# Identity products in TensorE's waits, later places for weight conversions, and two swaps at a handover

## The chip, the cores and the metric

One core of one Trainium2 chip runs the whole kernel in a single launch. The time is device microseconds of that core, as a median of runs. A core has five engines that run side by side, each through its own instructions in order: TensorE (PE, with its weight loads as PEld), VectorE (DVE), ScalarE (ACT), GpSimd (POOL) and SyncE (SP), which here issues most of the transfers. The transfers themselves run on 16 DMA engines.

## The reference

Three layers in sequence, on 4 batches of 448 tokens, 12 heads of 64:

```python
scores = q @ k.T / sqrt(64)                       # per batch and head
scores = einsum('bhij,hg->bgij', scores, w_pre)   # mix the heads
attn = softmax(scores - scores.max(-1))           # over j
attn = einsum('bhij,hg->bgij', attn, w_post)      # mix the heads again
x = (attn @ v), heads side by side                # 1792 x 768

h = x @ w_in                                      # 768 x 2048
x = (h - tanh(h)) @ w_out                         # 2048 x 768

logits = x @ phi                                  # 8 experts x 4 slots = 32
d = softmax(logits, over tokens); slot_input = d.T @ x
slot_out[e] = relu(slot_input[e] @ w1[e]) @ w2[e] # 768 x 1024 x 768, e < 8
out = softmax(logits, over slots) @ slot_out
```

All arrays are float32 on the chip, but for `w_in` and `w_out`, which come as float64 and are converted by the kernel on its own engines, as pairs of 32-bit words.

## The kernel before, in words

**Stage 1, attention** (`talking_heads`). Queries are cut into chunks of 120 (four a batch, the last of 88), and each chunk into slots of 10 queries with all 12 heads: 180 slots, 45 a batch. The main loop takes one step per slot. In step s it regroups the scores of slot s + 4 by a DMA from `S` to `D`, mixes the heads of slot s (`premix`, L317), normalizes slot s - 1, and mixes slot s - 3 again (`postmix`, L353). Everything else is planned into steps ahead of the loop, in the table `at`: scores of the next chunk ("head"), turns of k and q, products with v (`values`, L371), and transfers ("load"). The turns of the next batch's k (`k_pair`) lie in a stretch of 11 steps ahead of the batch: from `start[m - 1] - D_AHEAD` on, steps 20 to 30, 65 to 75 and 110 to 120. Their loads are up to six steps earlier.

Into the same steps go the 64 conversions of `w_in` and `w_out`, in pieces of 128 x 384. A conversion is a load by SyncE (L84 or L90), an absolute value on ScalarE (`absolute`, L46), four VectorE instructions (`exponent`, `head`, `tail`), an addition on GpSimd (L67) and a store by SyncE (L116). The planner walks through the pieces and chooses for each the step of the absolute value (a), of the exponent (x), the head (h) and the tail (e): a is the one of the steps t0 and t0 + 1 with the least planned load on ScalarE, where t0 is the later of `due` and of the head step of the piece before. The load is planned at the later of a - 4 and two steps after the tail of the piece three before, as there are three buffers.

**Handover.** The second function, `moe_and_slots`, is a generator: stage 1 calls `next` on it at the end of each of its last steps. There it loads and splits (`split_w`, `split_x`) the first weights and x into a rounded part and a rest, runs the first two products (`product`, L707), and begins their gates (`gate_act` on ScalarE, `gate_first` and `gate_last` on VectorE).

**Stage 2.** 64 steps, 16 blocks of hidden columns f for each of 4 batches: product of step t, gate of t - 1, turn of t - 2 (`turn_g`). In the first batch each step also loads and splits a block of `w_in`, saves it (`save_w`) for the other batches, and turns pieces of `w_out` (`turn_w`, two for each f, in all 32). The dictionary `pieces` says how many in which step; in steps 5, 9, 13 and 16 four turned blocks are folded with `phi` (`fold_first`, `fold_last`). The turns use the two banks r0 and r1 in alternation.

**Between stage 2 and the experts** (lines 1020 to 1076): the gate of the last step, its turn, the last logits (`logits`, L805), their mix (`mix_t`, L816), the exponentials (`slot_exp`), their turn (`slot_turn`, L872), the sums over tokens into slots (`slot_sum`, L881), `dt` (L1050), and the slots' inputs `si` (L1061) through `w_out`. **The experts** follow, with 32 weight loads of 1536 KB each (L647). Each load waits in a queue for a free "home" in SBUF: `give` adds one, `take` returns one after its use, and both call `load_expert`, which issues the next load. PSUM has eight banks; `h0`, `h1`, `h2` hold the products of three steps in turn.

Of the kernel before, what the change touches and what calls it, by code (L numbers as in the profile page):

```python
# [16 lines left out]
NB, NH, SEQ, HD = 4, 12, 448, 64  # L17
# [4 lines left out]
CHUNK = 120  # L22
# [96 lines left out]
def attention_chunks():  # L119
    out = []  # L120
    for b in range(NB):
        for i0 in range(0, SEQ, CHUNK):
            n = min(CHUNK, SEQ - i0)
            w = -(-n // IB)
            out.append((b, i0, n, [(o, len(range(o, n, w))) for o in range(w)]))
    return out
# [20 lines left out]
def talking_heads(tc, ident, q, k, v, w_pre, w_post, xd, box, follow):  # L147
    nc = tc.nc
    R = IB * NH
    chunks = attention_chunks()  # L150
    NC = len(chunks)
    slots = [(n, kk) for n in range(NC) for kk in range(len(chunks[n][3]))]
    NS = len(slots)
    D_AHEAD = 4
# [228 lines left out]
    start = [sum(len(c[3]) for c in chunks[:n]) for n in range(NC + 1)]  # L383
    at = {}

    def plan(kind, s, *a):
        at.setdefault((kind, s), []).append(a)
# [3 lines left out]
    def calm(kind, lo, hi):  # L391
        return min(range(lo, hi + 1), key=lambda s: (load[kind][s], s))
# [41 lines left out]
    pieces = box["early"]  # L434
    done = [0, 0, 0]
    t = 2
    for i, j in enumerate(pieces):
        due = 3 + i * (NS - D_AHEAD - 14) // len(pieces)
        t0 = max(t, due)
        a = calm("act", t0, t0 + 1)  # L440
        x = calm("dve", a + 1, a + 1 + (a <= due))
        load["dve"][x] += 0.54
        h = calm("dve", x, x + 1)
        load["dve"][h] += 0.47
        e = calm("dve", h, h + 1)
        load["dve"][e] += 0.74
        load["act"][a] += 0.41
        t = h
        done.append(e)
        plan("load", max(a - 4, done[i] + 2), cv.load, j)  # L450
        plan("act", a, cv.absolute, j)
        plan("dve", x, cv.exponent, j)
        plan("dve", h, cv.head, j)
        plan("dve", e, cv.tail, j)
        plan("load", e + 2, cv.store, j)
# [11 lines left out]
    warm = ps.tile([128, 128], FP32, tag="t", name="warm", bufs=2)  # L467
# [85 lines left out]
def moe_and_slots(tc, ident, xd, wi, wo, wo4, wis, consts, w1, w2, out, box):  # L553
    nc = tc.nc
# [3 lines left out]
    NE, _, F1 = w1.shape  # L558
# [27 lines left out]
    def bank(tag, shape, name):  # L586
        return bank_pool[tag].tile(shape, FP32, tag=tag, name=name)

    def r32(ap):
        return ap.bitcast(F32R)  # L590
# [14 lines left out]
    def unit(t):  # L605
        return ring[t % 3 if t < LAST else t % 2]
# [10 lines left out]
    def give(x, last=False):  # L617
        free.append((x, last))
        load_expert()
# [4 lines left out]
    def load_expert():  # L624
        if not queue or not free:
            return
        key = queue.pop(0)
        home = free.pop(0)
        x = home[0]
        kind, t = key  # L630
        if kind == "o":
            nc.sync.dma_start(out=x, in_=wo4[t])
        else:
            e, part = divmod(t, 4)
            i = part % 2
            if part < 2:
                n = KD // 2
                src = w1[e].rearrange("(p a) f -> p a f", p=128)[:, i * n:(i + 1) * n, :]
            else:
                src = w2[e].rearrange("(p a) f -> p a f", p=128)  # L640
                if by_column(e):
                    n = KF1
                    src = src[:, :, i * HALF:(i + 1) * HALF]
                else:
                    n = KF1 // 2
                    src = src[:, i * n:(i + 1) * n, :]
            nc.sync.dma_start(out=x.rearrange("p (a f) -> p a f", a=n), in_=src)  # L647
        ex_tiles[key] = home
# [22 lines left out]
    def split_w(t, eng):  # L671
        if t < NF:
            w = unit(t)
            nc.scalar.activation(out=r32(w[:, :, 0]), in_=w[:, :, 1], func=ACTF.Copy)
            eng.tensor_tensor(out=r32(w[:, :, 1]), in0=w[:, :, 1], in1=w[:, :, 0], op=ALU.subtract)  # L675
# [44 lines left out]
    def gate_act(t, beside=None):  # L720
        hp = hps[t]
        if t > 1:
            mem["sq"] = {t: bank(f"q{t % 2}", [128, SEQ], "sq")}
        sq, qd, mk, g = temps_of(t)
        nc.scalar.activation(out=sq, in_=hp, func=ACTF.Square)  # L725
        nc.scalar.activation(out=qd, in_=sq, func=ACTF.Square, bias=tshift)
        if beside:
            beside()
        nc.scalar.activation(out=g, in_=hp, func=ACTF.Tanh)
        nc.scalar.activation(out=mk, in_=sq, func=ACTF.Relu, bias=tlimit, scale=-1.0)  # L730
# [8 lines left out]
    def gate_last(t):  # L739
        hp = hps.pop(t)  # L740
        sq, qd, mk, g = temps_of(t)
        nc.vector.scalar_tensor_tensor(out=hp, in0=qd, scalar=TG_C, in1=hp, op0=ALU.mult, op1=ALU.mult)
        nc.vector.copy_predicated(out=g, mask=mk.bitcast(I32), data=hp)
# [10 lines left out]
    def turn_g(t):  # L754
        b, f = divmod(t, NF)
        if f % NG == 0:
            tok[b, f // NG] = quads.pop(0)
        g = g_of(t)
        x = turn_bank([JP, NR, 128], "gt")
        for r in range(NR):  # L760
            nc.tensor.transpose(out=x[:, r, :], in_=g[:, r * JP:(r + 1) * JP], identity=ident)  # L761
        i = f % NG
        dst = tok[b, f // NG][:JP].rearrange("p (r f) -> p r f", r=NR)[:, :, i * 128:(i + 1) * 128]
        nc.scalar.activation(out=dst, in_=x, func=ACTF.Copy)
# [44 lines left out]
    def logits_out(b):  # L809
        s = keep.tile([128, SEQ], FP32, tag="lp", name="lp")  # L810
        nc.scalar.activation(out=s, in_=lg.pop(b), func=ACTF.Copy)
        lp[b] = s

    def mix_t(b):
        xt = bank("lg", [128, SEQ], "lT")
        nc.tensor.matmul(xt, lhsT=sel.rearrange("p g s -> p (g s)"), rhs=lp[b], start=True, stop=True)  # L816
        lg[b] = xt
# [7 lines left out]
    def slot_exp(b):  # L825
        xt = lg.pop(b)
        nm = keep.tile([128, 1], FP32, tag="nm", name="nm")
        ng = keep.tile([128, 1], FP32, tag="ng", name="ng")
        et = keep.tile([128, SEQ], FP32, tag="et", name="et")
        sb = keep.tile([128, 1], FP32, tag="sb", name="sb")  # L830
        a = None
        nc.vector.tensor_reduce(out=nm, in_=xt, op=ALU.max, axis=AX.X)
        if b:
            nc.vector.tensor_tensor(out=nm, in0=nm, in1=run_m, op=ALU.max)
        nc.vector.tensor_scalar(out=ng, in0=nm, scalar1=-1.0, scalar2=None, op0=ALU.mult)
        nc.scalar.activation(out=et, in_=xt, func=ACTF.Exp, bias=ng, accum_out=sb)
        if b:
            a = keep.tile([128, 1], FP32, tag="al", name="al")
            nc.scalar.activation(out=a, in_=run_m, func=ACTF.Exp, bias=ng)
        es_in[b] = (a, et)  # L840
        runs[b] = (nm, sb)

    def slot_run(b):
        nm, sb = runs.pop(b)
        if b:
            nc.vector.tensor_scalar(
                out=run_s, in0=run_s, scalar1=es_in[b][0], scalar2=sb, op0=ALU.mult, op1=ALU.add)
        else:
            nc.vector.tensor_copy(out=run_s, in_=sb)
        nc.vector.tensor_copy(out=run_m, in_=nm)  # L850
# [17 lines left out]
    def slot_turn(b):  # L868
        a, et = es_in[b]
        xe = turn_bank([JP, NR, NSL], "etp")  # L870
        for r in range(NR):
            nc.tensor.transpose(out=xe[:, r, :], in_=et[:NSL, r * JP:(r + 1) * JP], identity=ident[:NSL, :NSL])  # L872
        es = keep.tile([JP, NR, NSL], FP32, tag="es", name="es")
        nc.scalar.activation(out=es, in_=xe, func=ACTF.Copy)
        es_in[b] = (a, es)
# [14 lines left out]
    pieces, folds = {}, {5: 0, 9: 1, 13: 2, 16: 3}  # L890
    todo = [(f, hf) for f in range(NF) for hf in range(2)]
    for n in range(3, NF + 1):
        m = 3 if n in (3, 4, 14, 15) else 2
        pieces[n], todo = todo[:m], todo[m:]

    def step(t):
# [89 lines left out]
    save_w(1)  # L986
    load_w(4)
    yield
    gate_act(1)
    yield  # L990
    split_w(2, nc.vector)
    while not box.get("go"):
        yield
    gate_first(1)
# [28 lines left out]
    xz = thp.tile([128, 2 * EXB], FP32, tag="xb", name="ex")  # L1023
    for i in range(2):
        give(xz[:, i * EXB:(i + 1) * EXB])
    gate_act(t - 1)
    gate_first(t - 1)
    turn_g(t - 2)
    gate_last(t - 1)
    turn_g(t - 1)  # L1030
    logits(b, NQ - 1)
    logits_out(b)
    temps.close()
    tmp = whole.enter_context(tc.tile_pool(name="m_tz", bufs=1, side="right", reuse_waits="tile"))
    give(tmp.tile([128, EXB], FP32, tag="tz", name="ex"))
    mix_t(b)
    slot_exp(b)
    slot_turn(b)
    slot_run(b)
    dgs = [bank(n, [128, FB], "sp") for n in ("h0", "h1", "q0", "q1")]  # L1040
    sr = keep.tile([128, NSL], FP32, tag="sr", name="sr")
# [15 lines left out]
    for k in range(NQ):  # L1057
        w = take(("o", k), NG)
        for hf in range(2):
            for g in range(NG):  # L1060
                nc.tensor.matmul(  # L1061
                    si[hf][NSL * g:NSL * g + NSL, :], lhsT=dgT[:, k * NG + g, :],
                    rhs=w[:, g, hf * HALF:(hf + 1) * HALF], start=(k == 0), stop=(k == NQ - 1))
# [245 lines left out]
```

## Time and profile before

| what | before |
|---|---|
| median of 3 runs | 962.18 us (961.09 to 964.81) |
| the profiled execution's own time | 964.55 us |
| its span, first to last instruction | 962.8 us |
| TensorE busy | 916.1 us, 95% |
| VectorE, ScalarE, GpSimd busy | 566.3, 571.1, 265.8 us |
| mean granted clock of TensorE | 0.973 |
| transfers | 230.22 MB, mean 239 GB/s |

The shares are over the whole span, and stages differ: about 490 us of attention, 340 us of stage 2, then 130 us of slots and experts. Matmuls are pipelined, so a busy TensorE is not one at its peak. The granted clock is a share of 2.4 GHz; 0.50 is 1.2 GHz.

### The profile page before, as it was taken

The numbers are of one execution on the slowest core, as the hardware profiler recorded it, in microseconds if no ns is written. First come the engines' busy times: TensorE is split into PE (matmuls) and PEld (weight loads), VectorE is DVE, ScalarE is ACT, GpSimd is POOL, SyncE is SP. The second block draws the span as 40 slices with busy tenths as digits, with TensorE's granted clock in tenths as the row PEclk, the third lists the DMA queues.
The fourth block names the chain that finished last, engine by engine and source line by source line (L and its number), as shares of the span: only waits on it lengthen the run. The fifth ranks groups of instructions, "written<-read, shape, count | busy, mean of one in ns | idle before, by whom it ended". The sixth has DMA issues, their size and how long they took to land.

```text
span 962.8 us, 19390 instructions
## 1 busy us (share of the span) xinstructions
PE 916.1 (95%) x6952; PEld 678.8 (71%) x6952; DVE 566.3 (59%) x1251; ACT 571.1 (59%) x1291; POOL 265.8 (28%) x467
## 2 busy tenths in 40 slices
PE   8899999989999999999989999999999999799985
PEld 6677777767777777777777777778778867444532
DVE  4576667766677766676455665667767666520103
ACT  4787777767776777776565675556556645401113
POOL 1464455544455545555422330000000000000000
PEclk9999999999999999999999999999999999868988
DMA  5897667977578876775548976796465448779997
GB/s 139 232 257 208 189 204 223 229 208 209 186 227 232 214 219 203 219 227 163 182 164 289 319 262 229 281 380 242 157 217 169 144 138 308 284 306 417 423 392 275
DMA packets 139634, 230.22 MB, mean 239 GB/s; under 512 B 58324, under 2 KB 118804, under 8 KB 134932
## 3 DMA queue, kind: packets, MB, share of 16 engines
q1 hardware_dynamic: 136976, 216.40, 69.5%
q10 hardware_dynamic: 2564, 12.60, 3.3%
q8 instruction: 56, 0.92, 0.4%
q14 instruction: 38, 0.31, 0.1%
HBM read 154.25 MB, written 36.18 MB: 198 GB/s over the span
## 4 chain that ended last, share of the span: by engine, by line
PE 81%; DMA 9%; ACT 4%; DVE 3%; issue 2%; POOL 0%; SPq 0%; ACTq 0%; POOLq 0%; DVEq 0%
PE hp L707 21%; PE pm L317 14%; PE tm L353 13%; PE vx L371 7%; PE sc L286 6%; PE gt L761 3%; PE h L1092 2%; PE sp L881 2%; PE so L1131 2%; DMA ex<-in_moe_w_dram 2%; DMA f<-in_moe_w_in_dram 2%; DMA rg<-wi 2%; DMA rg<-wis 2%; PE lgp L805 1%; PE tz L1110 1%
## 5 line engine op out<-in xcount | busy, mean ns | idle before, releaser
L353 PEld LDWEIGHTS tm<-wk,e 120*112 120x112 f32 (+1 forms) x1440 | 174.9, 178 | 70.8 <-issue 56.5
L319 DVE TENSOR_REDUCE mx<-pm 120x1 f32<-120x448 f32 x180 | 112.0, 622 | 124.5 <-PE pm L317 123.2
L317 PE MATMUL pm<-D,wpre 120*120 120x448 f32 x360 | 175.1, 569 | 6.8 <-ACT e L326 4.1
L353 PE MATMUL tm<-wk,e 120*112 120x120 f32 (+1 forms) x1440 | 177.5, 267 | 0.9 <-POOL wk L343 0.9
L356 ACT ACTIVATE aT<-tm 112x480 f32<-112x480 f32 x180 | 105.1, 584 | 111.3 <-PE tm L353 111.2
L343 POOL TENSOR_SCALAR wk<-wpost,rv 120x120 f32<-120x120 f32 x180 | 127.7, 709 | 136.1 <-PE tm L353 110.5
L707 PE MATMUL hp<-xa,rg 128*128 128x448 f32 x576 | 138.5, 380 | 0.6 <-POOL rg L675 0.6
L707 PE MATMUL hp<-xb,rg 128*128 128x448 f32 x576 | 133.5, 377 | 1.7 <-DMA rg<-wis 1.7
L707 PEld LDWEIGHTS hp<-xb,rg 128*128 128x128 f32 x576 | 103.9, 188 | 23.8 <-issue 14.1
L326 ACT ACTIVATE e<-pm,mx 120x448 f32<-120x448 f32 x180 | 113.4, 630 | 6.0 <-DVE rv L338 3.6
L707 PEld LDWEIGHTS hp<-xa,rg 128*128 128x128 f32 x576 | 102.3, 189 | 19.5 <-issue 11.5
L1103 POOL MEMSET tq<- 128x256 f32 x8 | 2.4, 311 | 339.0 <-PE sp L881 267.9
L294 ACT ACTIVATE S<-sc 120x448 f32<-120x448 f32 (+1 forms) x186 | 90.5, 543 | 3.1 <-PE sc L286 3.0
L371 PE MATMUL vx<-aT,vn 112*64 112x120 f32 (+1 forms) x1536 | 85.3, 265 | 1.8 <-DVE xs L376 1.8
L725 ACT ACTIVATE sq<-hp 128x448 f32<-128x448 f32 x62 | 32.8, 529 | 90.0 <-PE hp L707 89.7
L735 DVE SCALAR_TENSOR_TENSOR qd<-qd,sq 128x448 f32<-128x448 f32 x62 | 38.5, 621 | 79.3 <-ACT mk L730 79.0
L371 PEld LDWEIGHTS vx<-aT,vn 112*64 112x64 f32 x1536 | 75.0, 138 | 7.9 <-DVE xs L376 1.9
L317 PEld LDWEIGHTS pm<-D,wpre 120*120 120x120 f32 x360 | 51.6, 183 | 29.9 <-ACT e L326 15.9
L286 PE MATMUL sc<-khi,qT 64*120 64x448 f32 (+1 forms) x384 | 69.1, 388 | 0.8 <-DVE qT L269 0.8
L332 POOL TENSOR_SCALAR rv<-ss 120x1 f32<-120x1 f32 x180 | 41.2, 229 | 103.6 <-ACT e L326 92.3
L67 POOL TENSOR_TENSOR fa<-fa,f 128x384 f32<-128x384 f32 x64 | 65.9, 1030 | 5.3 <-DVE rv L338 0.2
L46 ACT ACTIVATE fa<-f 128x384 f32<-128x384 f32 x64 | 35.8, 559 | 18.8 <-DMA f<-in_moe_w_in_dram 15.3
(166 smaller groups left out, 1256.1 us busy)
## 6 DMA issues: line engine op xcount, KB each, us to landing
ex<-in_moe_w_dram SPq DMA_DIRECT2D x28, 1536.0 KB
D<-S SPq DMA_DIRECT2D x172, 210.0 KB
rg<-wis SPq DMA_DIRECT2D x34, 768.0 KB
f<-in_moe_w_in_dram SPq DMA_DIRECT2D x32, 384.0 KB
f<-in_moe_w_out_dram SPq DMA_DIRECT2D x32, 384.0 KB
wis<-rg ACTq DMA_DIRECT2D x16, 768.0 KB
rg<-wis SPq DMA_DIRECT2D x28, 384.0 KB
wi<-fa SPq DMA_DIRECT2D x32, 192.0 KB
```

The lines of the kernel that those rows point to most:

```text
L67: eng.tensor_tensor(out=out, in0=bits(a), in1=bits(p), op=ALU.add)
L286: nc.tensor.matmul(xs[e][0][:ni], lhsT=qT[n][s, l, p, :ni], rhs=kt[s], start=(i == 0), stop=(i == 2))
L294: nc.scalar.activation(out=dst, in_=xs[e][0][:ni], func=ACTF.Copy)
L317: nc.tensor.matmul(x[:r], lhsT=wpre[:r, :m, :], rhs=D_t.pop(s)[:r], start=True, stop=True)
L319: nc.vector.tensor_reduce(out=mx[:r], in_=x[:r], op=ALU.max, axis=AX.X, negate=True)
L326: nc.scalar.activation(out=e[:r], in_=pp_t.pop(s)[:r], func=ACTF.Exp, bias=mx_t.pop(s)[:r], accum_out=ss[:r])
L332: nc.gpsimd.tensor_scalar(out=rv[:r], in0=ss_t.pop(s)[:r], scalar1=EPS, scalar2=None, op0=ALU.add)
L343: nc.gpsimd.tensor_scalar(out=wk[:r], in0=wpost[:r], scalar1=ss_t.pop(s)[:r], scalar2=None, op0=ALU.mult)
L353: nc.tensor.matmul(x[:, c, :, :m], lhsT=e[:r, c * JP:(c + 1) * JP], rhs=wk[:r, :, :m], start=True, stop=True)
L356: nc.scalar.activation(out=attn_t[n][:, :, :, c0:c0 + m], in_=x[:, :, :, :m], func=ACTF.Copy)
L371: nc.tensor.matmul(x[64 * e:64 * e + 64, i, :ni], lhsT=nat_v[b, h // NP][:, h % NP, c, :], rhs=a[:, c, h, :ni], start=(c == 0), stop=(c == ...
L707: nc.tensor.matmul(hp, lhsT=r32(w[:, m, hl, cs]), rhs=r32(x_of(b, c, l)), start=(c == 0 and i == 0), stop=(c == KD - 1 and i == 2))
```

## The change

Four edits. The conversions of stage 1 get their due steps from a list of "quiet" steps, which leaves out the 11 steps in which the next batch's k is turned; the due steps inside that list are spread evenly, every second step. One turned piece of `w_out` moves from step 3 to step 5 of stage 2. In the generator, `split_w(2)` and `gate_act(1)` change places: the split is made one step of stage 1 earlier, the gate one later. And between stage 2 and the experts, TensorE multiplies the identity by itself 30 times, in five groups, into bank `h1`; the results are not read.

```diff
@@ talking_heads
     t = 2
+    busy = set()
+    for m in range(1, NC - 1):
+        if chunks[m][1] + CHUNK >= SEQ:
+            busy |= set(range(start[m - 1] - D_AHEAD, start[m - 1] - D_AHEAD + 11))
+    quiet = [x for x in range(4, NS - D_AHEAD - 11) if x not in busy]
     for i, j in enumerate(pieces):
-        due = 3 + i * (NS - D_AHEAD - 14) // len(pieces)
+        due = quiet[i * len(quiet) // len(pieces)]
         t0 = max(t, due)
@@ moe_and_slots
     for n in range(3, NF + 1):
-        m = 3 if n in (3, 4, 14, 15) else 2
+        m = 3 if n in (4, 5, 14, 15) else 2
         pieces[n], todo = todo[:m], todo[m:]
@@
     load_w(4)
     yield
+    split_w(2, nc.vector)
+    yield
     gate_act(1)
-    yield
-    split_w(2, nc.vector)
     while not box.get("go"):
         yield
@@
         give(xz[:, i * EXB:(i + 1) * EXB])
+    idle = bank("h1", [128, 128], "warm")
+
+    def warm(n):
+        for _ in range(n):
+            nc.tensor.matmul(idle, lhsT=ident, rhs=ident, start=True, stop=True)
+
+    warm(5)
     gate_act(t - 1)
     gate_first(t - 1)
     turn_g(t - 2)
+    warm(15)
     gate_last(t - 1)
     turn_g(t - 1)
     logits(b, NQ - 1)
     logits_out(b)
+    warm(2)
     temps.close()
     tmp = whole.enter_context(tc.tile_pool(name="m_tz", bufs=1, side="right", reuse_waits="tile"))
     give(tmp.tile([128, EXB], FP32, tag="tz", name="ex"))
     mix_t(b)
+    warm(7)
     slot_exp(b)
     slot_turn(b)
+    warm(1)
     slot_run(b)
```

## Rows read from the trace of the kernel before

**Rows 1.** The page: the chain that ended last, by engine.
```profile
PE 81%; DMA 9%; ACT 4%; DVE 3%; issue 2%; POOL 0%; SPq 0%; ACTq 0%; POOLq 0%; DVEq 0%
```

**Rows 2.** Windows: length, busy time (instructions) of each engine; clock, DMA share, GB/s.
```profile
core 0: us, PE busy (x) PEld busy (x) DVE busy (x) ACT busy (x) POOL busy (x), PEclk, DMA share, GB/s
...
140.00:160.00 20.00, 18.94 (x167) 14.21 (x163) 13.05 (x35) 14.22 (x36) 10.04 (x18) 1.00 0.74 211
...
180.00:200.00 20.00, 17.57 (x150) 13.63 (x148) 13.65 (x34) 13.87 (x35) 9.32 (x17) 0.96 0.95 239
200.00:220.00 20.00, 20.00 (x158) 14.88 (x155) 13.09 (x34) 13.35 (x34) 8.37 (x16) 0.96 0.72 196
...
300.00:320.00 20.00, 19.46 (x174) 15.07 (x175) 14.81 (x35) 15.05 (x39) 11.81 (x20) 1.00 0.94 237
...
880.00:900.00 20.00, 20.00 (x248) 10.38 (x242) 0.57 (x3) 1.19 (x2) 0.93 (x3) 1.00 1.00 419
```

**Rows 3.** Timeline of ScalarE: start, length, what, [idle before, its end].
```profile
162.80 0.56 ACT L46 ACTIVATE fa<-f 128x384 f32<-128x384 f32 x1
...
188.85 0.55 ACT L46 ACTIVATE fa<-f 128x384 f32<-128x384 f32 x1 [2.88 <-DMA f<-in_moe_w_in_dram]
...
195.24 0.54 ACT L46 ACTIVATE fa<-f 128x384 f32<-128x384 f32 x1 [2.71 <-DMA f<-in_moe_w_out_dram]
...
312.36 0.55 ACT L46 ACTIVATE fa<-f 128x384 f32<-128x384 f32 x1 [3.76 <-DMA f<-in_moe_w_in_dram]
```

**Rows 4.** Timeline of SyncE, the issuing of transfers in stage 1.
```profile
158.32 0.45 SPq L90 DMA_DIRECT2D f<-in_moe_w_in_dram  x1
...
183.17 0.62 SPq L116 DMA_DIRECT2D wo<-fa  x1
183.89 0.39 SPq L90 DMA_DIRECT2D f<-in_moe_w_in_dram  x1
...
188.85 0.37 SPq L84 DMA_DIRECT2D f<-in_moe_w_out_dram  x1
```

**Rows 5.** Timelines of VectorE and TensorE at the handover.
```profile
502.03 0.96 DVE L675 TENSOR_TENSOR rg<-rg 128x768 fp32r<-128x768 f32 x1 [1.84 <-ACT rg L674]
...
503.30 1.44 PE L371 MATMUL vx<-aT,vn 112*64 112x88 f32 x32 [1.77 <-DVE xs L376]
...
518.97 0.55 PE L774 MATMUL wt<-ident,ex 128*128 128x128 f32 x3 [0.92 <-ACT ex L778]
```

**Rows 6.** The chain in order of time, at the start and behind the handover.
```profile
1.43 4.64 PE warm L472 x20
...
508.90 7.81 DMA rg<-wi
```

**Rows 7.** Timeline of TensorE, an earlier slot sum and the stretch after stage 2.
```profile
616.52 1.07 PE L881 MATMUL sp<-tq,es 112*32 112x512 f32 x8
...
831.85 0.62 PE L761 MATMUL gt<-ident,g 128*112 128x128 f32 x4 [1.29 <-DVE g L743]
...
835.96 1.07 PE L761 MATMUL gt<-ident,g 128*112 128x128 f32 x4 [3.48 <-DVE g L743]
...
839.35 1.86 PE L816 MATMUL lT<-lp,sel 128*128 128x448 f32 x2 [0.66 <-ACT lp L811]
843.06 0.58 PE L872 MATMUL etp<-ident,et 32*112 32x32 f32 x4 [1.86 <-ACT et L836]
844.00 6.67 PE L881 MATMUL sp<-tq,es 112*32 112x512 f32 x32 [0.37 <-ACT es L874]
```

**Rows 8.** Windows between stage 2 and the experts.
```profile
836.00:844.00 8.00, 5.12 (x18) 1.76 (x18) 1.64 (x8) 2.32 (x6) 0.00 (x0) 0.50 1.01 432
844.00:850.00 6.00, 6.00 (x31) 1.36 (x32) 2.22 (x4) 0.00 (x0) 0.50 (x2) 0.50 0.47 199
847.00:851.00 4.00, 4.00 (x24) 0.98 (x16) 1.75 (x3) 0.00 (x0) 0.56 (x2) 0.61 0.01 3
851.00:855.00 4.00, 3.97 (x31) 3.83 (x30) 0.50 (x1) 0.00 (x0) 0.00 (x0) 0.82 0.81 261
```

**Rows 9.** Timeline of SyncE: the loads into the homes that the slot sums free.
```profile
850.79 0.81 SPq L647 DMA_DIRECT2D tq<-in_moe_w_dram  x2
```

## The prediction

> **What bounds the kernel now.** I read the chain of the whole run first: four fifths of it is TensorE and a tenth waiting for transfers, so a change counts where TensorE stands still or where a transfer ends last [rows 1]. Then the windows of 20 us. In stage 1 (to about 490 us) TensorE has no idle time in most of them; the exceptions are few: 1.06 us in 140 to 160, 2.43 us in 180 to 200, 0.54 us in 300 to 320. The granted clock of 0.96 in the two windows of 180 to 220 is 0.8 us less time at full speed in each, 1.6 us together. In 880 to 900 the DMA engines are at 1.00 of their time: the experts' weights set the pace there, not TensorE [rows 2].
>
> The waits of stage 1 come from one instruction. ScalarE takes the absolute value of a converted block (L46) in order, and stands until the block's load has landed: 2.88 and 2.71 us at the 25th and 26th conversion, 3.76 us at the 43rd, nothing at the 21st [rows 3]. SyncE issued those loads as late as 188.85 for a use at 195.24, 6.4 us; the quiet one was issued at 158.32 and used without a wait at 162.80, 4.5 us [rows 3, 4]. While the next batch's k is fetched, a load takes some 2 us longer.
>
> **Stage 1, the new places of the conversions.** The change keeps 64 conversions, their instructions and DMAs, and moves only their due steps. I worked through the loop of lines 437 to 455 with the costs written in it. Before, a due step comes every 2.5 steps; after, every second step outside three stretches (20 to 30, 65 to 75, 110 to 120). But `due` is only a lower bound: the start is at or after `max(t, due)`, and `t` is the head step of the conversion before, two or three steps after its start. At a due step in every two, the starts fall behind and can't catch up. So worked out, the starts around the second stretch are 60, 62, 64, 66, 69 (before: 60, 62, 64, 66, 69, 72, 74), around the third 105, 107, 109, 111, 114 (before: 105, 107, 109, 113, 115, 118). So the two that stalled, at 64 and 66, stay where they are, and the third stretch gets the same pair, 109 and 111, that it does not have now. The ones taken out (72, 74, 115, 118) are none of those that waited. Also, a load must wait for the buffer of the conversion three before, so at this pace its lead over its use shrinks to one step for 37 conversions (12 before).
>
> The prices. Second stretch: one more store and load stand ahead of the load for step 66 on SyncE's queue; such a pair is 183.17 to 184.28, 1.1 us [rows 4]. With the gap behind it I add 1.2 us to the stall, as if SyncE never stood idle there. The regroup transfers behind it on that queue are late by as much. Bounds: nothing is added and the stall goes, -2.43 and -1.6 for the clock, or +3 (two more pairs and their transfers). Third stretch: like the second now, 2.43 + 1.2 - 0.54 = 3.1 us, and half of the clock's 1.6 (whether the clock falls depends on how long TensorE stands), +3.9; bounds -0.5 and +5.5. First stretch (starts at 13, 15, 17, 19, then none to 32): +0.5, bounds 0 and +2.4. The other close starts: the wait in 140 to 160 is what such a series costs where it begins, 1.06 us [rows 2]; later ones in a series waited for nothing at the 21st conversion, so +0.4, bounds 0 and +2. VectorE, GpSimd and ScalarE have the same work, some 27% closer in the quiet steps; they are busy 13 to 15, 8 to 12 and 13 to 15 of 20 us [rows 2], which hides it. Sum of stage 1: 1.2 + 3.9 + 0.5 + 0.4 = **+6.0 us**.
>
> The Trainium skill ("DMA: Bandwidth & Descriptors", sections Bandwidth and Latency) gives a fixed cost of about 2 us and 341 GB/s at 1 MB; an estimate from it for 384 KB is 3.2 us, and by it a lead of one step would do and this term would be 0. The trace does not agree where k is fetched: 6.4 us stand from issue to use there [rows 3, 4].
>
> **The handover to stage 2.** The split of w 2 now goes ahead of gate 1 on ScalarE. Before, its VectorE half starts at 502.03, since its copy stood behind gate 1; the copies of the last values stand behind it and TensorE waits 1.77 us for them [rows 5]. After, the copy fits ahead of gate 1, whose input is not ready earlier anyway, so I take the 1.77 off. Moving the turn of one piece from step 3 to step 5 removes a wait of 0.92 us in step 4 [rows 5]. What is late next: the load of the next w, 7.81 us long, on which ScalarE stands ahead of the copies that free the turns' banks [rows 6]. It lands when the queue of weight loads and saves before it has drained, and these don't shrink; ScalarE stands until then whether TensorE came 1.8 us earlier or not. In step 5 the fold now comes right behind the third turned piece and may wait for its copy. So most is given back: **-0.4 us**, bounds -2.7 (all kept) and +0.5 (nothing kept, and a wait before the fold).
>
> **The identity products.** Between the last product and the experts TensorE waits 1.29, 3.48, 0.66, 1.86 and 0.37 us [rows 7], and behind the second works at half clock: 5.12 us busy in 836 to 844, 6.00 in 844 to 850, clock 0.50 in both [rows 8]. The 5, 15, 2, 7 and 1 products go into just these waits, into a bank that nothing else uses until `dgs`. Ten of them took 4.64 us at the start of the kernel, 0.46 each [rows 6]. That is a price at the lower level: at 0.50 the mix of 448 columns takes 1.86 us [rows 7, 8], or 0.53 for 128. At the upper level it is 0.23, and the five groups take 1.16, 3.48, 0.46, 1.62 and 0.23 us: all fit, the second one just. Bounds 0.23 and 0.46. At the first wait the clock is still full (four transposes take 0.62 us behind it and 1.07 behind the second [rows 7]), and TensorE would be busy through all five, as in 880 to 900, where the clock is 1.00 [rows 2], so I take 0.23.
>
> Then the work in 836 to 844 halves, up to -2.5, and so do the slot sums: 32 instructions in 6.67 us at half clock, 8 of an earlier batch in 1.07 at full, ends included [rows 7], so some 3.4, -3.3. About -5.6 us at the slot sums' end. That alone is not the gain, since the end is set by weights. But the slot sums release two homes, and their loads are issued at 850.79 [rows 9], while the DMA engines have stood empty since 847: share 0.01 in 847 to 851, 0.81 in 851 to 855 [rows 8], 3.96 + 0.76 = 4.7 us lost. Issued at 845.2, they follow on the loads before without a gap; some 0.9 us are in hand. From there on the stream is full in the rows [rows 2], and what feeds it comes as much earlier. The term is **-4.7 us**; the rest of 5.6 is hidden by the stream. Bounds: -4.9 and 0 (if the clock falls all the same).
>
> **The sum.** -4.7 - 0.4 + 6.0 = +0.9 us on the profiled execution's 964.55 us (a span of 962.8 and 1.75 around it), which lies 2.4 above the median. Moved to the median of 962.18: **963 us**. What a measurement of this kernel can tell from no change is about 0.5%, 957.4 to 967.0.
>
> **The rivals.**
> - *The conversions cost nothing, or their stalls go* (chance 0.31). For it: the quiet load of 4.5 us was in time with a lead of one step [rows 3, 4], the DMA engines have more room without four conversions per stretch, and waits of up to 3.76 us on ScalarE cost TensorE only 0.54 [rows 2, 3]. Then -4.7 - 0.4 = 957; with the stall of 180 to 200 and its clock gone too, -4.1 more, 953. By the Trainium skill's figure above it is this case. Against it: the starts 64 and 66 do not move.
> - *Every stretch stalls as the second does now, and each close series costs its 1 us* (0.17; the one that ends slower). The place is L46 with a lead of one step during the fetch of k; it decides once loads there take 6.4 us or more. First +2.4, second +3, third +5.5, series +2: 12.9 - 5.1 = +7.8, 970 us. For it: the starts 109 and 111. Against it: the load of the 43rd, late by 3.76 us, took only 0.54 from TensorE [rows 2, 3].
> - *The change doesn't hold the clock or its products run at the lower level* (0.09). At 0.46 the second group takes 7 us in a wait of 3.48 and pushes the chain; the term of -4.7 goes to 0 or above: 968 us. Against it: the clock is full when the first group starts [rows 7].
>
> **How the numbers follow.** My case has 0.43, with its own range of 958 to 967. The range over the cases leaves out the rivals' ends: 953.5 to 970. Faster by over 0.5%: the first rival, 0.30. Slower: the second and part of the third and of mine, 0.27. Within: 0.43.
>
> **What would show it.** In the changed profile: conversions at the 23rd and 24th place with ScalarE idle 2 us or more before L46 (step 64 and 66), and a TensorE gap of over 2 us near 315 where there is 0.54 now; no such gaps would prove the first rival. The gap of 1.77 before the last values gone, the load of w landing near 516 still. Granted clock 1.00 from 831 to the slot sums' end, the two loads issued 13 to 14 us behind the transposes at the first wait (19 now), and the DMA engines never empty from there to the last weights. What would make it wrong above all: stage 1 of 4 us more or less.

## The result, and the profile after

| | median (lowest to highest) | runs |
|---|---|---|
| before | 961.63 us (957.89 to 964.81) | 6 |
| after | 967.49 us (965.85 to 970.64) | 6 |

The ratio is 1.0068, with a 95% interval of 1.0038 to 1.0097 (that of the two medians is 1.0061): the changed kernel is slower. The time lies in the forecast range, 4.5 us above the forecast itself; of the three directions it took the one that had been given 0.27. The profiled execution of the changed kernel has a span of 968.6 us, 5.8 more than before.

Where the span changed can be followed by three marks: the start of stage 2's product 0, its product 16 (the first that reads `xb`), and the end of its last product.

| profiled execution | product 0 starts | product 0 to 16 | product 16 to the last one's end | from there to the end |
|---|---|---|---|---|
| before | 490.60 | 99.95 | 240.00 | 132.27 |
| after | 498.80 | 103.78 | 239.87 | 126.14 |

So stage 1 is 8.2 us later, the handover loses 3.8 and the tail gains 6.1. Forecast were +6.0, -0.4 and -4.7. These are differences of two single executions; how far such marks vary stands in the table behind the experiments.

Stage 1. The waits of ScalarE ahead of L46, SyncE's issues that they hang on (L84 loads from `w_out`, L90 from `w_in`), and TensorE's gaps in the changed kernel, in timelines:
```profile
55.08 0.54 ACT L46 ACTIVATE fa<-f 128x384 f32<-128x384 f32 x1 [3.36 <-DMA f<-in_moe_w_in_dram]
...
186.72 0.55 ACT L46 ACTIVATE fa<-f 128x384 f32<-128x384 f32 x1 [4.00 <-DMA f<-in_moe_w_out_dram]
...
192.59 0.54 ACT L46 ACTIVATE fa<-f 128x384 f32<-128x384 f32 x1 [2.02 <-DMA f<-in_moe_w_in_dram]
...
311.93 0.55 ACT L46 ACTIVATE fa<-f 128x384 f32<-128x384 f32 x1 [5.29 <-DMA f<-in_moe_w_in_dram]
```
```profile
46.46 0.39 SPq L90 DMA_DIRECT2D f<-in_moe_w_in_dram  x1
...
181.65 0.42 SPq L84 DMA_DIRECT2D f<-in_moe_w_out_dram  x1
...
185.29 1.26 SPq L90 DMA_DIRECT2D f<-in_moe_w_in_dram  x1
```
```profile
56.75 1.35 PE L317 MATMUL pm<-D,wpre 120*120 120x448 f32 x2 [3.38 <-ACT e L326]
...
313.61 1.10 PE L317 MATMUL pm<-D,wpre 120*120 120x448 f32 x1 [2.65 <-ACT e L326]
```
A load issued at 181.65 lets ScalarE go on at 186.72, one issued at 185.29 at 192.59: 5.1 and 7.3 us, the second more than the 6.4 of [rows 3, 4]. The load of the 5th conversion, issued at 46.46, lets it go on at 55.08: 8.6 us, the longest of those that it stood for. The stall near 313 is there, as forecast, and one near 56 that I had put at half a microsecond. The signs named were waits at the 23rd and 24th conversion (starts 64 and 66); they are 2.02 and 1.58 us. The longest wait in both later stretches is one start earlier than I had worked out: 4.00 us at 186.72 (start 62) and 5.29 us at 311.93 (start 107). Windows of the changed kernel, same columns as [rows 2]:
```profile
180.00:200.00 20.00, 16.35 (x131) 12.04 (x130) 13.70 (x33) 12.12 (x32) 9.05 (x17) 1.00 0.96 250
300.00:320.00 20.00, 17.35 (x129) 12.98 (x128) 13.04 (x33) 11.52 (x30) 9.14 (x16) 0.91 0.83 225
320.00:340.00 20.00, 18.96 (x167) 14.60 (x168) 14.29 (x34) 13.65 (x35) 10.10 (x19) 1.00 0.59 168
510.00:520.00 10.00, 6.92 (x55) 6.07 (x52) 3.40 (x8) 4.29 (x7) 3.65 (x2) 0.90 0.93 278
520.00:530.00 10.00, 10.00 (x47) 8.86 (x47) 4.86 (x9) 4.81 (x9) 1.85 (x1) 0.75 0.68 232
836.00:844.00 8.00, 7.76 (x47) 6.91 (x47) 4.82 (x9) 4.20 (x8) 0.00 (x0) 1.00 0.12 28
844.00:850.00 6.00, 5.50 (x47) 4.24 (x45) 2.97 (x5) 2.27 (x5) 0.00 (x0) 1.00 0.96 401
850.00:870.00 20.00, 18.60 (x163) 11.72 (x162) 5.78 (x14) 2.06 (x6) 0.56 (x2) 0.99 0.97 390
```
In 180 to 200 TensorE is idle for 3.65 us in four gaps of at most 1.48 us (2.43 us in one gap before), and the clock stays at 1.00; in 300 to 320 for 2.65 in one gap (0.54 before), and there it falls.

The handover. The wait of 1.77 us of [rows 5] is gone. In its place TensorE stands 3.08 us for the output weights `wo`, which the chain of waits shows with a transfer of 6.82 us. Timeline of TensorE, then the chain in order of time:
```profile
519.01 0.87 PE L779 MATMUL wt<-ident,ex 128*128 128x128 f32 x3 [3.08 <-DMA ex<-wo]
```
```profile
512.05 6.82 DMA ex<-wo
```
In the kernel before, the same turns in the timeline of TensorE, and two windows:
```profile
510.76 0.52 PE L774 MATMUL wt<-ident,ex 128*128 128x128 f32 x3 [1.07 <-DMA ex<-wo]
```
```profile
510.00:520.00 10.00, 8.33 (x51) 7.33 (x52) 5.36 (x10) 6.91 (x13) 3.67 (x2) 1.00 0.83 289
520.00:530.00 10.00, 9.62 (x62) 6.93 (x64) 5.87 (x11) 6.23 (x12) 1.85 (x1) 1.00 0.82 271
```
SyncE began to issue the four loads of `wo` 13.25 us behind the start of product 0, and they were there at 20.2; before, it began at 15.2 behind it and they were there at 20.2 as well (TensorE waited 1.07 us for them at 510.76). So the earlier issue brought nothing. The DMA engines were busy 0.96 of the time meanwhile (512 to 519), which I take for the reason; no run tried it. Then the clock falls: 0.90 and 0.75 in the windows above, where before it was 1.00.

The tail, timeline of TensorE and the two loads of [rows 9]:
```profile
843.84 3.51 PE L1035 MATMUL warm<-ident 128*128 128x128 f32 x30
...
853.67 3.64 PE L886 MATMUL sp<-tq,es 112*32 112x512 f32 x32
```
```profile
857.42 0.80 SPq L652 DMA_DIRECT2D tq<-in_moe_w_dram  x2
```
Fifteen identity products (two instructions each) take 3.51 us, 0.234 each: the forecast price at the upper level. The clock is 1.00 in 836 to 850 above, and 1.00 in 842 to 869, the slot sums take 3.64 us instead of 6.67 [rows 7], and the loads go out 14.0 us behind the transposes at the first wait, at 843.40 (18.9 before). The DMA share of 0.97 in 850 to 870 has no empty stretch any more; the 0.12 in 836 to 844 is the first one, ahead of the end of the last product.

### The profile page after: what moved, and what is told of

It is laid out like the page before. It is cut to its first block, busy times and chain, and to the rows that moved or that the text cites. A ratio compares the mean times of both kernels' runs of the same rounds, so it can differ in the third digit from the quotient of the medians.

```text
span 968.6 us, 19522 instructions
## 1 busy us (share of the span) xinstructions
PE 921.2 (95%) x7012; PEld 685.7 (71%) x7012; DVE 567.2 (59%) x1251; ACT 571.5 (59%) x1291; POOL 266.7 (28%) x467
## 4 chain that ended last, share of the span: by engine, by line
PE 70%; DMA 17%; ACT 5%; DVE 4%; issue 2%; POOL 1%; SPq 0%; ACTq 0%; POOLq 0%; DVEq 0%
PE hp L712 19%; PE pm L317 12%; PE tm L353 11%; PE vx L371 7%; PE sc L286 6%; DMA ex<-in_moe_w_dram 5%; DMA f<-in_moe_w_in_dram 5%; PE gt L766 3%; DMA f<-in_moe_w_out_dram 2%; PE sp L886 2%; ACT e L326 1%; DMA rg<-wis 1%; DMA wis<-rg 1%; PE h L1108 1%; PE lgp L810 1%
## 5 line engine op out<-in xcount | busy, mean ns | idle before, releaser
L712 PEld LDWEIGHTS hp<-xa,rg 128*128 128x128 f32 x576 | 103.8, 191 | 20.3 <-issue 11.5
L326 ACT ACTIVATE e<-pm,mx 120x448 f32<-120x448 f32 x180 | 113.5, 631 | 7.6 <-DVE rv L338 5.5
L46 ACT ACTIVATE fa<-f 128x384 f32<-128x384 f32 x64 | 35.9, 561 | 38.8 <-DMA f<-in_moe_w_in_dram 21.6
```

Of the source, the lines that this page charges most:

```text
L326: nc.scalar.activation(out=e[:r], in_=pp_t.pop(s)[:r], func=ACTF.Exp, bias=mx_t.pop(s)[:r], accum_out=ss[:r])
L712: nc.tensor.matmul(hp, lhsT=r32(w[:, m, hl, cs]), rhs=r32(x_of(b, c, l)), start=(c == 0 and i == 0), stop=(c == KD - 1 and i == 2))
```

## The experiments

Each ratio is to the kernel before on the same chip, with its 95% interval; microseconds behind it are that share of some 961. The ratios of the medians differ from these by up to 0.0013 (in E2 957.87 to 961.37 us, 0.9964). E1 to E4 ran on one chip, E5 to E8 and E12 on a second, E9 to E11 on a third. In the edits, "..." stands for lines left out.

**E1, the new due steps alone.**
```diff
...
-        due = 3 + i * (NS - D_AHEAD - 14) // len(pieces)
+        due = quiet[i * len(quiet) // len(pieces)]
```


> Only the new due steps of the conversions; the handover and the waits before the experts are as before. Mine (loads with a lead of one step land late in three stretches, and TensorE waits behind L46): the last product of stage 1 ends 8 us later than before, as in the changed kernel, in gaps of 3.4, 3.7 and 3.7 us near 57, 188 to 200 and 314 to 325, and the clock falls at one or two of them; the handover adds nothing, so the time is +7 to +8.5 us (ratio 1.007 to 1.009). Rival (the conversions are neutral, and stage 1 is late in the changed kernel's one profile by where the clock happened to fall): stage 1 within 3 us of before, time within 0.3%. Rival for the handover (it loses 3.8 us because stage 1 ends 8 us later, not by the swap): this kernel's handover loses 3 to 4 us too, time +11 to +12 us.

Measured: 1.0055 (1.0023 to 1.0088), +5.3 us, below the 7 to 8.5 that I expected. The gaps are those of the changed kernel, smaller in this execution (1.63 us near 55, 1.0, 0.4 and 0.6 near 186 to 196, 1.3, 0.4 and 1.7 near 308 to 319). The loss of stage 1 is that of the due steps. The handover loses nothing (99.08 us). In this execution product 0 starts only 1.4 us later than before, so that alone doesn't rule out a late stage 1 as the cause of the handover's loss; E4 does.

**E2, the identity products alone.**
```diff
...
+    warm(5)
     gate_act(t - 1)
...
+    warm(15)
     gate_last(t - 1)
...
```


> Only the 30 identity products. Mine (the clock is held from the first wait on, and the gain is limited to what the DMA engines lose by standing empty): stage 1 and the handover as before, -4.7 to -6.1 us at the end (ratio 0.9935 to 0.995), the clock at 1.00 until the slot sums' end, no second empty stretch of the DMA engines near 848 to 852. Rival (the tail gained 6.1 us in the changed kernel because a later stage 2 let the weights run ahead of the products): -2 to -4 us. Rival (the clock falls all the same where stage 2 ends at another time): 0.

Measured: 0.9976 (0.9951 to 1.0002), -2.3 us: less than forecast, and by itself not to be told from no change. The number is one that the first rival gives (the tail gains by a later stage 2), but the traces don't bear it out: in E4 stage 2 ends 13.6 us earlier than in the changed kernel, and the tail is as short (125.66 and 126.14 us). The clock is held through the waits and falls right behind, windows:
```profile
836.00:844.00 8.00, 7.54 (x60) 4.93 (x63) 2.88 (x10) 2.33 (x6) 0.00 (x0) 1.00 1.01 430
844.00:850.00 6.00, 6.00 (x58) 3.96 (x51) 2.99 (x4) 0.00 (x0) 0.56 (x2) 1.00 0.93 363
850.00:870.00 20.00, 18.18 (x132) 8.89 (x131) 2.50 (x8) 2.11 (x5) 0.00 (x0) 0.74 1.00 411
```

**E3, the two edits of the handover alone.**
```diff
-        m = 3 if n in (3, 4, 14, 15) else 2
+        m = 3 if n in (4, 5, 14, 15) else 2
...
-    gate_act(1)
-    yield
     split_w(2, nc.vector)
+    yield
+    gate_act(1)
```


> Only the two edits of the handover: split ahead of gate 1, and one turned piece moved from step 3 to step 5. Stage 1 as before. My prediction's term was -0.4 us. What the changed kernel's trace speaks for: product 2 starts 1.9 us earlier, but TensorE then stands 3 us before step 3's turns (for the transfer of the output weights), the clock falls, and product 15 is 3 to 4 us later than before: time +3 to +4 us (ratio 1.003 to 1.004). Rival (the loss there is that of a late stage 1 only): product 15 at -0.4 to -2 us, time -0.2%.

Measured: 1.0006 (0.9979 to 1.0032), not the +3 to +4 us that I expected. In the trace product 2 starts 1.96 us earlier from product 0, TensorE then stands 3.04 us for `wo`, and product 16 is 1.6 us later. What the two edits cost in time is 0.6 us with 2.5 either way, and whether the wait is the swap's or the moved piece's E6 tells.

**E4, the change without the new due steps** (the edits of E2 and E3; the diff is against the changed kernel).
```diff
...
-        due = quiet[i * len(quiet) // len(pieces)]
+        due = 3 + i * (NS - D_AHEAD - 14) // len(pieces)
```


> The change without the new due steps. Mine, if the parts add up: handover +3.8, tail -6.1, so -2 us (ratio 0.998). Rival (the handover's loss comes from the late stage 1): handover -0.4 to -2, so -6.5 to -8 us (ratio 0.992 to 0.993). Rival (the tail's gain needs the late stage 2): handover +3.8, tail -3, so +1.

Measured: 0.9965 (0.9933 to 0.9996), -3.4 us. TensorE stands 3.99 us for `wo`, and products 0 to 16 take 102.89 us, though product 0 starts at 486.22, earlier than in any other kernel with three buffers: the handover's loss doesn't come from a late stage 1. Beside E3 the products are worth 0.4% here.

**E5, the new due steps with a fourth buffer for a conversion.** It asks whether the loads are late for want of a buffer or because the stretches are denser.
```diff
-        self.bufs = 3
+        self.bufs = 4
...
-    done = [0, 0, 0]
+    done = [0, 0, 0, 0]
...
-        due = 3 + i * (NS - D_AHEAD - 14) // len(pieces)
+        due = quiet[i * len(quiet) // len(pieces)]
```


> The new due steps as in the first experiment, with four buffers for a conversion instead of three, so that a load may go out a conversion earlier. Mine (the loss of the new due steps is loads with a lead of one step): the gaps near slots 16, 65 to 68, 98 and 110 to 113, 8 to 12 us together with the three buffers, fall to 3 us or less, and the time to that of before or below, -2 to 0 us (ratio 0.998 to 1.000). Rival (the loss is that of the denser stretches, in which the engines and the DMA engines have more to do): the gaps stay, +5 us (1.005).

Measured: 0.9935 (0.9901 to 0.9969), -6.2 us, more than I expected. TensorE's gaps between 50 and 470 us shrink to three of 1.27, 0.80 and 0.60 us. How long ScalarE stood for a load ahead of L46 from 40 to 480 us (the view of that line: us, times) before,
```profile
  DMA f<-in_moe_w_in_dram: 15.3, 5
  DMA f<-in_moe_w_out_dram: 3.4, 2
```
in the changed kernel,
```profile
  DMA f<-in_moe_w_in_dram: 21.6, 8
  DMA f<-in_moe_w_out_dram: 14.8, 7
```
and in E5:
```profile
  DMA f<-in_moe_w_in_dram: 0.7, 1
```

**E6, the swap of split and gate alone**, the turned pieces as before.
```diff
-    gate_act(1)
-    yield
     split_w(2, nc.vector)
+    yield
+    gate_act(1)
```


> Only the split of w 2 ahead of gate 1; the pieces stay at step 3. Mine (the output weights land when the queues have drained, so the 1.77 us gained come back as a wait of 3 us or more before the turns of step 3): product 2 starts 1.8 us earlier, measured from product 0, product 4 no earlier than before, product 15 at 0 to +2 us; the time within 0.2% of before. Rival (it is the moved piece that loses): product 15 at -1.8 to -1 us.

Measured: 1.0006 (0.9981 to 1.0031). TensorE stands 3.46 us for `wo`; product 16 is 1.25 us later than before. The wait is the swap's, not the moved piece's.

**E7, the handover's edits with the turns of step 3 later in its product** (the diff is against E3).
```diff
-            on(1, turn_w, *ws[0])
+            on(5 if t == 3 else 1, turn_w, *ws[0])
...
-            on(3, turn_w, *ws[1])
+            on(6 if t == 3 else 3, turn_w, *ws[1])
```


> Both edits of the handover, and the two turns of step 3 four and three chunks later in its product (2 us), so that the product runs while the output weights arrive. Mine (the wait for the output weights is what eats the gain): the gap before step 3's turns falls from 3 to 4 us to 1 to 2 us, the clock doesn't fall there, and product 15 is 1 to 2 us earlier than before, measured from product 0: time -1 to -2 us (ratio 0.998 to 0.999). Rival (what is late next is the load of the next w or a bank, so the gain goes there): product 15 at 0 to +3, as with the two edits alone.

Measured: 0.9997 (0.9972 to 1.0022), no gain, and product 16 at 102.52 us. The rival is right. The wait for `wo` is gone, and others stand in its place; the longest, in the timelines of TensorE and of ScalarE:
```profile
523.98 0.55 PE L774 MATMUL wt<-ident,ex 128*128 128x128 f32 x3 [2.00 <-ACT tq L764]
```
```profile
521.64 0.84 ACT L674 ACTIVATE rg<-rg 128x768 fp32r<-128x768 f32 x1 [3.29 <-DMA rg<-wi]
```
ScalarE's copies of the turned pieces stand behind the split of the next w, and that behind its load. This is the wait that the prediction had named; in the change itself `wo` hides it.

**E8, the identity products without the group of 15** (the diff is against E2).
```diff
-    warm(15)
+    warm(0)
```


> The identity products without the group of 15 in the longest wait: 5, 0, 2, 7 and 1. Mine (the clock is lost in the wait of 3.48 us, which stays empty): the clock falls there as before, the first slot sums at half clock, 0 to -1 us (ratio 0.999 to 1.000). Rival (the five ahead of it are enough to hold the clock): as with all 30, -2.5 to -4.5 us (0.9955 to 0.9975).

Measured: 0.9958 (0.9931 to 0.9985), no worse than with all 30. Neither theory is quite right. In the wait of 3.47 us that stays empty the clock does fall, but it is back for the slot sums, which take 3.64 us. Windows, and the timeline of TensorE:
```profile
838.00:848.00 10.00, 7.86 (x50) 4.69 (x54) 3.47 (x11) 2.32 (x6) 0.00 (x0) 0.83 1.00 428
```
```profile
840.50 1.72 PE L805 MATMUL lgp<-g,wphi 128*32 128x448 f32 x8
...
846.94 3.64 PE L881 MATMUL sp<-tq,es 112*32 112x512 f32 x32
```
Without products the clock was 0.50 from 836 to 850 [rows 8]. What the fall costs is ahead of the sums (1.72 us for `lgp`, 0.96 in the changed kernel). The two loads behind them go out 16.2 us behind the last product's end, 15.0 with all 30 products, 18.8 to 20.2 without any: most of the gain at these loads is kept. The tail, 127.61 us, is the longest of the seven with products, by 0.5 us.

**E9, the kernel before with four buffers.**
```diff
-        self.bufs = 3
+        self.bufs = 4
...
-    done = [0, 0, 0]
+    done = [0, 0, 0, 0]
```


> The kernel before with four buffers for a conversion instead of three, and its own due steps. Mine (a load that may go out a conversion earlier lands in time everywhere): ScalarE's waits for the loads ahead of L46, 18.7 us in 7 places before, fall to 2 us or less, stage 1 gains the 2.4 us of TensorE's gaps that they cause and now and then a fall of the clock: -2 to -4 us (ratio 0.996 to 0.998). If it gains as much as with the new due steps (0.9935), those steps are worth nothing; if it gains nothing, the gain there was that of the steps, and the buffer only lets it out.

Measured: 0.9923 (0.9893 to 0.9953), -7.4 us, more than I expected. ScalarE's waits for loads ahead of L46 are gone altogether, and TensorE is never idle in the windows where [rows 2] had gaps:
```profile
180.00:200.00 20.00, 20.00 (x177) 15.23 (x175) 15.48 (x39) 14.47 (x37) 10.76 (x20) 1.00 0.91 245
300.00:320.00 20.00, 20.00 (x177) 15.16 (x176) 13.38 (x33) 14.14 (x35) 9.52 (x17) 1.00 0.90 240
```
The gain of E5 is that of the buffer. The new due steps add nothing to it (0.9935 and 0.9923, on two chips), and may cost: the gaps of 1.27, 0.80 and 0.60 us that E5 keeps are not here.

**E10, the whole change with four buffers** (the diff is against the changed kernel).
```diff
-        self.bufs = 3
+        self.bufs = 4
...
-    done = [0, 0, 0]
+    done = [0, 0, 0, 0]
```


> The whole change, with four buffers for a conversion. Mine (the buffers were what the change lacked; the parts add up): the sum of what was measured for the parts, -0.65% for steps and buffers, -0.3% for the products, 0 to +0.2% for the handover: ratio 0.990 to 0.993, -7 to -9 us. Rival (what the change lost beyond the sum of its parts lies elsewhere, in the parts together): 0.996 or above.

Measured: 0.9929 (0.9899 to 0.9960), as expected. The change as a whole is no loss once the loads are in time, and no gain either: four buffers alone measured 0.9923 on the same chip (E9). TensorE stands 3.21 us for `wo`. In stage 1 it now stands for the regrouped scores D, once in the second and once in the third stretch in which the next batch's k is turned; timeline:
```profile
185.78 0.98 PE L317 MATMUL pm<-D,wpre 120*120 120x448 f32 x2 [1.32 <-DMA D<-S]
...
306.60 0.98 PE L317 MATMUL pm<-D,wpre 120*120 120x448 f32 x2 [2.64 <-DMA D<-S]
```

**E11, E10 without the handover's edits** (the diff is against E10).
```diff
-        m = 3 if n in (4, 5, 14, 15) else 2
+        m = 3 if n in (3, 4, 14, 15) else 2
...
+    gate_act(1)
+    yield
     split_w(2, nc.vector)
-    yield
-    gate_act(1)
```


> As the run before it, without the two edits of the handover. Mine (there the 1.95 us gained at the last values come back as a wait for the output weights, and now and then a fall of the clock): the same to 2 us faster than with them, ratio 0.989 to 0.992; product 15 at 1 to 3 us less, measured from product 0. Rival (the swap gains once stage 1 is in time): 2 us slower than with them.

Measured: 0.9915 (0.9889 to 0.9940). Products 0 to 16 take 99.84 us (102.71 with the edits); the difference in time, 0.14%, is within the intervals. The waits for D in these two stretches are here too (2.83 us at 190.10, 0.72 at 309.82).

**E12, four buffers and the identity products, all else as before.**
```diff
-        self.bufs = 3
+        self.bufs = 4
...
+    warm(5)
     gate_act(t - 1)
...
```


> Four buffers for a conversion and the identity products, with the due steps and the handover of before. Mine (buffers and products act in different stages and add up; the new due steps and the swap give nothing on top): no wait of ScalarE for a load ahead of L46, product 15 some 95 us behind product 0 as in the kernels without the swap, and 126 to 127.5 us from the last product's end to the end of the span, where kernels without the products have 129 to 130.5: ratio 0.988 to 0.990. Rival (the products gain nothing once stage 1 is in time, as the steps with four buffers and products, 0.9915, against the buffers alone, 0.9923, could be read): 0.992 or above.

Measured: 0.9884 (0.9839 to 0.9929), 950.40 us beside 961.47: the lowest ratio of the study, as forecast, though its interval overlaps those of E9 and E11. Product 0 starts at 482.32, product 16 at 99.64 behind it, and 126.68 us are left at the last product's end. Between 50 and 470 us TensorE has no gap of over 0.25 us, and none in E9: with four buffers and the old due steps these waits are not there.

The three marks over all profiled executions, the changed kernel and the one before included (means, lowest to highest, number of executions):

| what differs | with | without |
|---|---|---|
| product 0 starts: new due steps, three buffers | 495.4 (491.97, 498.80) | 490.7 (486.22 to 495.27; 7) |
| the same, four buffers | 485.7 (481.72 to 488.94; 3) | 480.7 (479.13, 482.32) |
| products 0 to 16: the swap | 102.4 (101.20 to 103.78; 6) | 100.3 (99.08 to 102.71; 8) |
| last product's end to the end: identity products | 126.6 (125.66 to 127.61; 7) | 130.0 (128.93 to 132.27; 7) |

## Why the prediction was right or wrong, point by point

**Stage 1, +6.0: mechanism right, the sum partly by luck.** E1 measures +5.3 (2.2 to 8.5). The starts at 64 and 66 stalled as worked out, and 109 and 111 too. The single stretches were off, read from the starts of the slots in the two profiled executions: the second cost nothing on balance (forecast +1.2; its gaps grew by 1.2 us, but the clock did not fall there), the third some 4.9 (forecast +3.9), and the first, forecast at +0.5, has a gap of 3.38 us and lost 5.0. The close starts around slots 95 and 150 lost another 1.3 and 0.9 (forecast +0.4 together). Against that stood some 3.6 us at the very start that I had not foreseen: a wait of 2.19 us for a transfer of D at the tenth slot, with a fall of the clock, is 0.18 in the changed kernel. Timeline of TensorE before:
```profile
40.78 1.42 PE L317 MATMUL pm<-D,wpre 120*120 120x448 f32 x2 [2.19 <-DMA D<-S]
```
So parts that were off by -3.6 to +4.5 us came to a sum that was off by 2.2 in the trace (8.2) and by 0.7 in time. E5 shows that the loads' lead is the main cause: with one more buffer ScalarE's waits for loads fall from 36.4 us (21.6 and 14.8) to 0.7, and the loss is gone. Whether it is the whole cause stays open, since E5's rival, the denser stretches, is not settled. Against kernels that have four buffers and the old steps, the new steps are 0.1% (E5 beside E9) and 0.3% slower (E11 beside E12), both within the intervals; product 0 starts 5.0 us later in the mean; and in E5, E10 and E11 TensorE keeps gaps, of up to 2.83 us, around the three stretches of k that E9 and E12 don't have. The Trainium skill's figure ("DMA: Bandwidth & Descriptors", sections "Bandwidth" and "Latency and other measured facts"), 3.2 us by my estimate for such a load, is not borne out here either: 5.1 and 7.3 us from issue to use.

**Handover, -0.4: the step that failed.** The 1.77 us were taken off as worked out, and the 0.92 us of step 4 became 0.74 us a step later (at 534.60); the sentence that ScalarE's wait for "the load of the next w" is late next named the wrong transfer. The loads of `wo` are late first. In the changed kernel and before they land 20.2 us behind the start of product 0, with the swap and without it, so that the gain of 1.95 us comes back as a wait of 3.0 to 4.0 us for them in the five kernels that have the swap and the turns at their old place (1.07 before). That the full DMA engines fix this landing is argued from their share, not tried. My upper bound, "nothing kept, and a wait before the fold", +0.5, left out that the longer stand can cost the clock too: +3.8 in the changed kernel, +2.1 in the mean over the executions, whose ranges overlap (E8, without the swap, has 102.71 us). By time alone the two edits cost 0.6 us (E3), which can't be told from nothing. Which part of the 2.1 us is the clock's was only read from the windows, not tried.

**Identity products, -4.7: the mechanism right, the size off.** They run at the upper level, hold the clock, and the DMA engines' second empty stretch is gone. But the tail of the one execution that I reckoned from was the longest of the seven without products, 132.27 us; the mean is 130.0, and 126.6 with them: -3.4, and by time -2.3 (E2) and -3.9 (E4 beside E3). In that execution the clock came back later: the two loads behind the slot sums go out 20.2 us behind the last product's end, 18.8 to 19.8 in the six others without products, and 15.0 with all 30. That the gain is not the whole 5.6 us of the chain holds, and E8 fits it: half the products, with a fall of the clock between them, do as well by time within the intervals. The granted clock of all timed runs says the same: 0.982 in the mean with the products alone (E2), 0.977 without, 0.005 of 960 us or, by estimate, some 5 us at the higher level, of which 2.3 show in the time.

**The sum.** +5.3 (E1), +0.6 (E3) and -2.3 (E2) make +3.6 us; the change measured +6.5 (3.7 to 9.3). The difference of 2.9 us is within the intervals; whether the parts disturb each other beyond that stays open. By these numbers the forecast's +0.9 fell short by 5.6 us: 2.4 for the products, 1.0 for the handover, 2.9 that no part accounts for, less 0.7 that stage 1 was put too high. By the spans of the two profiled executions (+5.8) it would be 4.2 for the handover and 2.2 for stage 1, less 1.4 for the tail; one execution of each can't decide between the two. That the time lies in the range is right; the direction, given 0.27, was not the likeliest. Of the rivals, the first (conversions cost nothing) is refuted by E1; the second (every stretch stalls, 970 us) is half right, since the first stretch does stall, but E1's +5.3 is far from its 12.9; the third did not happen.

## What to carry to other kernels

A buffer count sets how early a load can go out, whatever the schedule says: before moving due dates, count the lead of each load over its use, and compare it with the longest time from issue to use in the trace. When a stall is removed ahead of a transfer that lands no earlier for it, as `wo` here, the gain moves to that transfer; look for it by subtracting the gain from the slack of every transfer behind the stall. And a term worked out from a stretch where the clock falls should be checked on a second execution, since that stretch may be an unusual one: here it made a term of 4.7 us out of some 3.4. And an edit is to be compared with a kernel that differs in that edit alone: the new due steps look harmless in E5 beside the old kernel, and bring nothing beside E9.

## What was not expected of the hardware

Executions whose stage 1 is the same differed by 9 us there: product 0 started between 486.22 and 495.27. The wait at the tenth slot alone was 0.84 to 3.77 us. And the clock fell in some and not in others behind the same gap: behind the wait of 1.77 us before the last values, first the kernel before, then E2, windows:
```profile
500.00:510.00 10.00, 7.92 (x99) 6.86 (x93) 5.67 (x10) 4.30 (x8) 1.83 (x1) 1.00 0.90 296
```
```profile
500.00:510.00 10.00, 8.23 (x112) 7.29 (x111) 6.71 (x12) 4.35 (x7) 1.82 (x1) 0.83 0.92 313
```
So the prediction's reason for taking half of the clock's 1.6 us, that the fall depends on how long TensorE stands, is not shown by these rows alone. The fourth buffer gained more (7.4 us) than the idle time of TensorE that I put down to late loads in the rows before (2.43 us, and 1.6 of the clock): product 0 of E9 starts 11.5 us earlier than the mean of the seven kernels with three buffers and the same steps (10.0 in the mean of E9 and E12). The gaps of half a microsecond behind L326 at 156, 279 and 398 us before are gone with it too, and the clock is 1.00 throughout between 100 and 470 us; which of these made up the rest was not taken apart.
